# Six equal groups, and the first group's output layer moved in between its input layer's slices

## The chip, the cores and the metric

One core of one Trainium2 chip. The metric is the device time of one execution in microseconds (us); it is quoted as the median of several executions, with the extremes where they matter. The span of a profile, from the first to the last instruction, is 1.75 to 1.8 us shorter than the time of the same execution. Each execution also has a mean granted clock of TensorE (1.0 is full speed).

Engines: PE is TensorE, DVE is VectorE, ACT is ScalarE, POOL is GpSimd, SP is SyncE.

## The reference, cut to what matters

```
state = gamma*state + k[t] (x) v[t];   y[t] = scale * q[t] @ state     # retention, 4 x 8 heads, 768 steps of 64
x = y as (3072, 512)
h = x @ w_in                            # 512 -> 2048
g = h + sin(alpha*h)**2 / (alpha + 1e-9)
out = g @ w_out                         # 2048 -> 512
```

The kernel works in 24 chunks of 128 tokens (4 sequences of 6 chunks). Attention of a chunk has four steps on PE: **T** (transposes of q and k), **A** (scores), **M** (state read and aT times v, into py) and **S** (state update). VectorE copies T's result (qkT), masks A's (aT) and multiplies M's by a decay table (xT). Then come the two layers, for a group of chunks together. The input layer has 16 slices f of 128 columns: four matmuls, a sine and a square, an add (gT). The output layer has 16 matmuls for every chunk, one for each f. I call one such 128x512 matmul an **out**. A group needs its attention before its input layer, and its gT before its outs.

## The kernel before

```python
sizes = [4, 2, 4, 4, 4, 4, 2]                       # chunks in a group

load_w_in(0); load_w_in(1)                          # quarters, some lines put together
load_w_out(0); load_w_in(2); load_w_out(1); load_w_in(3); load_w_out(2); load_w_out(3)

def stage_A(j):
    qkT = st["qkT", j]
    pa = psum.tile([128, 2, NP, 128], F32, name="pa", tag="pa")             # the size of two outs
    ...                                             # eight matmuls
    nc.vector.tensor_mul(aT, pa, mask)              # one mask of 128x1024

def ff_in(g, f, square, cols=None):
    ph = psum.tile([128, hi - lo], F32, name="ph", tag="mm", bufs=4)
    ...                                             # four matmuls
    nc.scalar.activation(out=s, in_=ph, func=ACTF.Sin, scale=alpha_sb[:, f:f + 1])
    if square == "A":
        nc.scalar.activation(out=s, in_=s, func=ACTF.Square)
    else:
        nc.vector.tensor_mul(s, s, s)
    return lambda: nc.vector.scalar_tensor_tensor(gT[g][:, f, lo:hi], s, rec_alpha[:, f:f + 1], ph, ...)

# group 0: three chunks first (f 0 to 5), the fourth chunk e3 in between, with filler matmuls
for f in range(early):
    adds.append(ff_in(0, f, "AADAAA"[f], (0, n3)))
    ...                                             # T, A of e3 between, and dummy matmuls (idle_work)
stage_M(e3)
...
phase(0, [outs of chunk 0], {}, "AD", range(early, FF))
outs = out_pieces(0, (1, 2, 3))                     # the other three chunks' outs: 48
...
# attention of the two chunks of group 1, filled with outs of group 0
fill(7); stage_T(P[4]); scale_v(P[4], nc.vector)
fill(5); stage_A(P[4]); keep_S(P[0], stage_S(P[0]))
fill(5); stage_T(P[5]); scale_v(P[5], nc.vector)
fill(5); stage_A(P[5]); stage_M(P[4])
fill(6); stage_M(P[5]); fill(3)
phase(1, outs, {...}, "A")                          # group 1 (two chunks), the last 19 outs, attention of group 2
```

Of the kernel before, what the change touches and what calls it, by code (L numbers as in the profile page):

```python
# [15 lines left out]
def kernel(  # L16
# [29 lines left out]

    order = [b * NCH for b in range(B)]
    order += [b * NCH + c for b in range(B) for c in range(1, NCH)]
    sizes = [4, 2, 4, 4, 4, 4, 2]
    assert sum(sizes) == NJ  # L50
    NG = len(sizes)
    groups = [order[sum(sizes[:g]):sum(sizes[:g + 1])] for g in range(NG)]
# [37 lines left out]
    def load_w_in(i):  # L90
        nc.gpsimd.dma_start(out=w_in[:, :, i * fw:(i + 1) * fw], in_=w_in_v[:, :, i * fw:(i + 1) * fw])

    def load_w_out(i):
        nc.gpsimd.dma_start(out=w_out[:, i * fo:(i + 1) * fo, :], in_=w_out_v[:, i * fo:(i + 1) * fo, :])
# [16 lines left out]
    def scale_v(j, eng):  # L111
        eng.tensor_mul(raw["v", j], raw["v", j], kg[:, j % NCH, :, None].to_broadcast([128, H, D]))  # L112
# [2 lines left out]
    load_chunk(order[1])  # L115
    load_chunk(order[2])
    load_w_in(0)
    load_w_in(1)
    load_chunk(order[3])
    load_w_out(0)  # L120
    load_w_in(2)
    load_w_out(1)
    load_w_in(3)
    load_w_out(2)
    load_w_out(3)
    for j in order[4:7]:
        load_chunk(j)

# [35 lines left out]
    def decay_table(c):  # L164
        nc.vector.tensor_mul(qg[:, c], qg[:, 0], step[:, c, :, None].to_broadcast([128, NP, C]))
# [24 lines left out]
    def stage_T(j):  # L190
        pt = psum.tile([128, 2 * NP, 128], BF16, name="pt", tag="ty")
        st["qkT", j] = work.tile([128, 2 * NP, 128], BF16, name="qkT", tag="qkT", bufs=6)
        for i in range(2):
            for p in range(NP):
                nc.tensor.transpose(pt[:, i * NP + p, :],  # L195
                                    raw["qk"[i], j][:, 2 * p:2 * p + 2, :].rearrange("p h d -> p (h d)"), ident)
        nc.vector.tensor_copy(st["qkT", j], pt)  # L197
# [3 lines left out]
        st["qkT", j] = work.tile([128, 2 * NP, 128], BF16, name="qkT", tag="qkT", bufs=6)  # L201
        nc.sync.dma_start_transpose(out=st["qkT", j], in_=raw["qk", j].rearrange("p i h d -> p (i h d)"))

    def stage_A(j):
        qkT = st["qkT", j]
        pa = psum.tile([128, 2, NP, 128], F32, name="pa", tag="pa")
        for p in range(NP):
            for e in range(2):
                r = slice(64 * e, 64 * e + 64)
                nc.tensor.matmul(pa[:, e, p, :], qkT[r, NP + p, :], qkT[r, p, :],  # L210
                                 start=(p == 0), stop=True, skip_group_check=True)
        aT = work.tile([128, 2, NP, 128], BF16, name="aT", tag="aT", bufs=2)
        m = dec.rearrange("p e n t -> p (e n) t") if j % NCH == 0 else mask_bc
        nc.vector.tensor_mul(aT.rearrange("p e n t -> p (e n) t"), pa.rearrange("p e n t -> p (e n) t"), m)  # L214
        st["aT", j] = aT

    def stage_S(j):
# [44 lines left out]
    def ff_in(g, f, square, cols=None):  # L262
        n = sizes[g] * C
        lo, hi = cols or (0, n)
        if g not in gT:
            gT[g] = work.tile([128, FF, n], BF16, name="gT", tag="gT", bufs=2)
        ph = psum.tile([128, hi - lo], F32, name="ph", tag="mm", bufs=4)
        s = work.tile([128, hi - lo], F32, name="s", tag="s", bufs=4)
        for i in range(KS):
            nc.tensor.matmul(ph, w_in[:, i, f * 128:(f + 1) * 128], xT[g][:, i, lo:hi],  # L270
                             start=(i == 0), stop=(i == KS - 1))
        nc.scalar.activation(out=s, in_=ph, func=ACTF.Sin, scale=alpha_sb[:, f:f + 1])  # L272
        if square == "A":
            nc.scalar.activation(out=s, in_=s, func=ACTF.Square)  # L274
        else:
            nc.vector.tensor_mul(s, s, s)  # L276
        return lambda: nc.vector.scalar_tensor_tensor(  # L277
            gT[g][:, f, lo:hi], s, rec_alpha[:, f:f + 1], ph, op0=ALU.mult, op1=ALU.add)

# [1 line left out]
    po = {}  # L281
    end = (NG - 1, sizes[-1] - 1)

    def ff_out(g, ts, f):
        if f == 0:
            po[g, ts] = psum.tile([128, d_model], F32, name="po", tag="mm", bufs=4)
        nc.tensor.matmul(po[g, ts], gT[g][:, f, ts * C:(ts + 1) * C], w_out[:, f, :],  # L287
                         start=(f == 0), stop=(f == FF - 1))
        if f == FF - 1:
            o_sb = work.tile([128, d_model], F32, name="o_sb", tag="o_sb", bufs=3)  # L290
            o_dram = out_view[:, groups[g][ts], :]
            if (g, ts) == end:
                h = d_model // 2
                nc.vector.tensor_copy(o_sb[:, :h], po[g, ts][:, :h])
                nc.scalar.copy(o_sb[:, h:], po[g, ts][:, h:])
            else:
                nc.scalar.copy(o_sb, po[g, ts])  # L297
            nc.sync.dma_start(out=o_dram, in_=o_sb)

    def out_pieces(g, tss):  # L300
        return [lambda ts=ts, f=f: ff_out(g, ts, f) for ts in tss for f in range(FF)]
# [5 lines left out]
    def idle_work(n):  # L307
        for _ in range(n):
            nc.tensor.matmul(spare["ps"], warm[:, :128], warm, start=True, stop=True)  # L309
# [47 lines left out]
    def phase(g, outs, att, squares, slots=range(FF)):  # L357

        no, n0, done = len(outs), len(slots), 0
        for n, f in enumerate(slots):  # L360
            add = ff_in(g, f, squares[f % len(squares)])
            for fn in att.get(f, ()):
                fn()
            add()
            while done < no * (n + 1) // n0:
                outs[done]()
                done += 1

    def T(j):
        return lambda: stage_T(j)  # L370

    def X(j):
        return lambda: turn(j)
# [13 lines left out]
    def SK(j):  # L387
        return lambda: keep_S(j, stage_S(j))


    n3, early = 3 * C, 6
    adds = []
    for f in range(early):
        adds.append(ff_in(0, f, "AADAAA"[f], (0, n3)))
        if f == 0:
            decay_table(3)
        if f in (1, 2):
            adds.pop(0)()
        if f == 3:
            idle_work(2)  # L400
            stage_T(e3)
            idle_work(1)
            adds.pop(0)()
        if f == 4:
            stage_A(e3)
            adds.pop(0)()
    idle_work(2)
    adds.pop(0)()
    stage_M(e3)
    adds.pop(0)()  # L410
    idle_work(3)
    for f in range(early):
        add = ff_in(0, f, "AD"[f % 2], (n3, 4 * C))
        if f > 1:
            ff_out(0, 0, f - 2)
        add()
    decay_table(4)
    scale_v(e0, nc.vector)
    for t in s_bd:
        nc.vector.memset(t, 0.0)  # L420
    decay_table(5)
    P = order
    phase(0, [lambda f=f: ff_out(0, 0, f) for f in range(4, FF - 2)], {}, "AD", range(early, FF))
    outs = out_pieces(0, (1, 2, 3))
    outs[9:9] = [lambda f=f: ff_out(0, 0, f) for f in range(FF - 2, FF)]

    def fill(n):
        for _ in range(n):
            outs.pop(0)()


    for n in range(7, NJ + 3):
        if n > 8:
            scale_v(order[n - 3], nc.gpsimd)
        if n < NJ:
            load_chunk(order[n])
        if n in (13, 15, 17):
            scale_v(order[(n - 11) // 2], nc.gpsimd)

    fill(7)  # L440
    stage_T(P[4])
    scale_v(P[4], nc.vector)
    fill(5)
    stage_A(P[4])
    keep_S(P[0], stage_S(P[0]))
    fill(5)
    stage_T(P[5])
    scale_v(P[5], nc.vector)
    fill(5)
    stage_A(P[5])  # L450
    stage_M(P[4])
    fill(6)
    stage_M(P[5])
    fill(3)
    phase(1, outs,
          {0: [T(P[6]), X(P[8])], 2: [A(P[6])], 3: [T(P[7])], 4: [X(P[9])], 6: [A(P[7]), M(P[6])], 8: [X(P[10])],
           10: [A(P[8]), M(P[7])], 12: [X(P[11])], 13: [A(P[9]), M(P[8]), SK(P[9] - 1)], 15: [M(P[9])]}, "A")
    for g in range(2, NG):
        att = {}
        if g + 1 < NG:  # L460
            js = groups[g + 1]
            for i, j in enumerate(js):
                a = i * FF // len(js)
                n = P.index(j) + 2
                if n < NJ:
                    att.setdefault(a + 2, []).append(X(P[n]))
                att.setdefault(a + 1, []).append(A(j))
                if i > 0:
                    att[a + 1].append(M(js[i - 1]))
                if j % NCH == 1:  # L470
                    att[a + 1].append(SK(j - 1))
            att.setdefault(FF - 2, []).append(M(js[-1]))
        phase(g, out_pieces(g - 1, range(sizes[g - 1])), att, "A")
    for fn in out_pieces(NG - 1, range(sizes[-1])):
        fn()


# [1 line left out]
_INS = ['q', 'k', 'v', 'moe_w_in', 'moe_w_out', 'moe_alpha']  # L479
_OUTS = [((3072, 512), 'float32')]  # L480
# [25 lines left out]
```

## Time and profile before

| | before |
|---|---|
| time, median of 4 fast runs beside the changed kernel | 221.68 us (221.38 to 221.96) |
| span of its profile | 220.3 us |
| mean clock of its runs, all studies | 0.995 to 1.0 |
| PE's need, counted from the starts of its matmuls | 192.2 us |

The page of the kernel before cuts the span into 40 slices of 5.5 us; a digit is the busy share in tenths:

```profile
PE   7698889999999999999999999999999999999992
DVE  5586798876896768854565565556554455333300
PEclk9999999999999999999999999999999999999999
```

After the sixth slice (33 us) PE is full everywhere but in the last; DVE is full in two slices only. A stage whose PE is full can still have the chain of another engine hidden below it (from 39.45 to 49.92 us PE is busy for all 10.47 us and VectorE for 8.27), and that is what the change disturbs.

### The profile page before, as it was taken

The numbers are of one execution on the slowest core, as the hardware profiler recorded it, in microseconds if no ns is written. First come the engines' busy times: TensorE is split into PE (matmuls) and PEld (weight loads), VectorE is DVE, ScalarE is ACT, GpSimd is POOL, SyncE is SP. The second block draws the span as 40 slices with busy tenths as digits, with TensorE's granted clock in tenths as the row PEclk, the third lists the DMA queues.
The fourth block names the chain that finished last, engine by engine and source line by source line (L and its number), as shares of the span: only waits on it lengthen the run. The fifth ranks groups of instructions, "written<-read, shape, count | busy, mean of one in ns | idle before, by whom it ended". The sixth has DMA issues, their size and how long they took to land.

```text
span 220.3 us, 4282 instructions
## 1 busy us (share of the span) xinstructions
PE 209.3 (95%) x1661; PEld 106.9 (49%) x1661; DVE 132.3 (60%) x218; ACT 164.8 (75%) x322; POOL 90.1 (41%) x105
## 2 busy tenths in 40 slices
PE   7698889999999999999999999999999999999992
PEld 2444433457664545544455444445444444556540
DVE  5586798876896768854565565556554455333300
ACT  7678777538999999798778778778768877777720
POOL 8965336899999989779510000000000000000000
PEclk9999999999999999999999999999999999999999
DMA  9999999999999999999994145145111101111121
GB/s 127 154 193 191 207 207 163 152 201 155 170 151 145 156 149 185 125 162 175 160 128 71 27 95 72 28 97 74 24 49 51 48 0 51 48 48 48 52 89 54
DMA packets 99509, 24.67 MB, mean 112 GB/s; under 512 B 92304, under 2 KB 96416, under 8 KB 99488
## 3 DMA queue, kind: packets, MB, share of 16 engines
q0 software_dynamic: 77024, 13.37, 83.5%
q1 hardware_dynamic: 22464, 11.02, 26.1%
q8 instruction: 13, 0.21, 0.4%
q14 instruction: 8, 0.07, 0.1%
HBM read 27.27 MB, written 6.29 MB: 152 GB/s over the span
## 4 chain that ended last, share of the span: by engine, by line
PE 79%; DVE 9%; ACT 6%; DMA 2%; issue 2%; SPq 0%; ACTq 0%
PE po L287 36%; PE ph L270 32%; PE pa L210 3%; DVE aT L214 3%; DVE gT L277 3%; PE py L244 3%; ACT s L272 3%; PE py L248 2%; DMA k<-in_k_dram 2%; ACT s L274 2%; PE spare L309 1%; PE ps L224 1%; DVE s L276 1%; DVE xT L255 1%; PE pt L195 1%
## 5 line engine op out<-in xcount | busy, mean ns | idle before, releaser
L277 DVE SCALAR_TENSOR_TENSOR gT<-s,rec_alpha,ph 128x512 bf16<-128x512 f32 (+3 forms) x118 | 75.7, 645 | 67.1 <-ACT s L274 66.3
L287 PE MATMUL po<-w_out,gT 128*128 128x512 bf16 x384 | 101.9, 380 | 1.3 <-DVE gT L277 0.9
L270 PE MATMUL ph<-xT,w_in 128*128 128x512 bf16 (+3 forms) x472 | 101.5, 339 | 1.3 <-DVE gT L277 0.7
L272 ACT ACTIVATE s<-ph,alpha_sb 128x512 f32<-128x512 f32 (+3 forms) x118 | 71.3, 606 | 31.9 <-PE ph L270 31.9
L270 PEld LDWEIGHTS <-w_in 128*128 128x128 bf16 x472 | 45.4, 98 | 46.3 <-issue 4.6
L274 ACT ACTIVATE s<-s 128x512 f32<-128x512 f32 (+3 forms) x109 | 60.3, 553 | 3.5
L287 PEld LDWEIGHTS <-gT 128*128 128x128 bf16 x384 | 35.5, 98 | 38.4 <-DVE gT L277 4.1
L112 POOL TENSOR_TENSOR vr<-vr,kg 128x512 bf16<-128x512 bf16 x21 | 22.2, 1067 | 8.5 <-DMA vr<-in_v_dram 8.5
L214 DVE TENSOR_TENSOR aT<-pa,mask 128x1024 bf16<-128x1024 f32 x20 | 24.4, 1221 | 0.1
L83 POOL DMA_DIRECT2D vr<-in_v_dram x24 | 21.7, 905 | 3.3 <-DMA w_in<-in_moe_w_in_dram 1.7
L83 POOL DMA_DIRECT2D qkr<-in_q_dram x23 | 21.3, 927 | 3.7 <-DMA w_out<-in_moe_w_out_dram 1.6
L83 POOL DMA_DIRECT2D qkr<-in_k_dram x23 | 20.4, 888 | 3.7 <-DMA w_out<-in_moe_w_out_dram 3.3
L297 ACT COPY o_sb<-po 128x512 f32<-128x512 f32 x23 | 13.2, 574 | 6.2 <-PE po L287 6.1
L231 ACT CAST s_bd<-ps 64x256 bf16<-64x256 f32 x40 | 14.4, 360 | 3.5 <-PE ps L224 2.9
L255 DVE TENSOR_TENSOR xT<-py,qg 128x512 bf16<-128x512 f32 x20 | 13.7, 684 | 2.3 <-PE py L248 2.2
L309 PE MATMUL spare<-warm 128*128 128x512 bf16 x36 | 11.4, 430 | 1.2 <-DVE warm L131 1.2
L210 PE MATMUL pa<-qkT 64*128 64x128 bf16 x192 | 9.5, 219 | 0.7 <-DVE qkT L197 0.3
L210 PEld LDWEIGHTS <-qkT 64*128 64x128 bf16 x192 | 5.4, 94 | 9.6 <-issue 6.8
L248 PE MATMUL py<-aT,vr 128*64 128x128 bf16 x192 | 9.5, 219 | 0.5 <-DVE rec_alpha L347 0.2
L244 PE MATMUL py<-qkT,s_bd 128*64 128x128 bf16 x160 | 8.3, 225 | 0.2 <-DVE xT L255 0.2
L248 PEld LDWEIGHTS <-vr 128*64 128x64 bf16 x192 | 6.9, 110 | 1.5 <-issue 1.1
L244 PEld LDWEIGHTS <-s_bd 128*64 128x64 bf16 x160 | 5.2, 109 | 4.0 <-issue 1.9
(58 smaller groups left out, 70.0 us busy)
## 6 DMA issues: line engine op xcount, KB each, us to landing
out_dram<-o_sb SPq DMA_DIRECT2D x24, 256.0 KB, 2.3
vr<-in_v_dram POOLq DMA_DIRECT2D x24, 128.0 KB, 7.5
qkr<-in_q_dram POOLq DMA_DIRECT2D x23, 128.0 KB, 7.8
qkr<-in_k_dram POOLq DMA_DIRECT2D x23, 128.0 KB, 7.7
w_in<-in_moe_w_in_dram POOLq DMA_DIRECT2D x4, 512.0 KB, 11.0
w_out<-in_moe_w_out_dram POOLq DMA_DIRECT2D x4, 512.0 KB, 14.7
q<-in_q_dram SPq DMA_DIRECT2D x1, 256.0 KB, 3.4
k<-in_k_dram SPq DMA_DIRECT2D x1, 256.0 KB, 4.9
```

What stands on the lines that cost most here:

```text
L83: nc.gpsimd.dma_start(out=t, in_=chunk_of(src, j))
L112: eng.tensor_mul(raw["v", j], raw["v", j], kg[:, j % NCH, :, None].to_broadcast([128, H, D]))
L210: nc.tensor.matmul(pa[:, e, p, :], qkT[r, NP + p, :], qkT[r, p, :], start=(p == 0), stop=True, skip_group_check=True)
L214: nc.vector.tensor_mul(aT.rearrange("p e n t -> p (e n) t"), pa.rearrange("p e n t -> p (e n) t"), m)
L244: nc.tensor.matmul(py[r, p, :], s_bd[c % 2][:, p, r], qkT[:, p, :], start=(p == 0), stop=True, skip_group_check=True)
L248: nc.tensor.matmul(py[64 * e:64 * e + 64, p, :], vs[:, 2 * p + e, :], aT[:, e, p, :], start=(c == 0 and p == 0), stop=True, skip_group_che ...
L255: nc.vector.tensor_mul(x, py, qg[:, c])
L270: nc.tensor.matmul(ph, w_in[:, i, f * 128:(f + 1) * 128], xT[g][:, i, lo:hi], start=(i == 0), stop=(i == KS - 1))
L272: nc.scalar.activation(out=s, in_=ph, func=ACTF.Sin, scale=alpha_sb[:, f:f + 1])
L274: nc.scalar.activation(out=s, in_=s, func=ACTF.Square)
L277: return lambda: nc.vector.scalar_tensor_tensor(gT[g][:, f, lo:hi], s, rec_alpha[:, f:f + 1], ph, op0=ALU.mult, op1=ALU.add)
L287: nc.tensor.matmul(po[g, ts], gT[g][:, f, ts * C:(ts + 1) * C], w_out[:, f, :], start=(f == 0), stop=(f == FF - 1))
```

## The change

Its intent: equal groups of four, so that every weight load of PE serves 512 columns; the outs of group 0 directly behind the slices f that they need, in tiles of PSUM (the pool to which both kernels let PE write; one for a 128x512 fp32 result is called a bank here) that attention will only want later; half of group 1's squares on GpSimd, so that ScalarE has room. The core of it:

```diff
-    sizes = [4, 2, 4, 4, 4, 4, 2]
+    sizes = [4] * 6
-    load_w_out(0); load_w_in(2); load_w_out(1); load_w_in(3); ...
+    load_w_out(0) ahead of e3; then w_out and w_in quarters by turns
-            nc.vector.tensor_mul(s, s, s)
+            (nc.vector if square == "D" else nc.gpsimd).tensor_mul(s, s, s)
-    ... f 0 to 5 for three chunks, T(e3), A(e3) and dummy matmuls between, M(e3) ...
+    own = (0, 1, 2)
+    wide = psum.tile([128, 2, d_model], F32, name="wide", tag="pa")          # attention's banks
+    po[0, 0], po[0, 1] = wide[:, 0], wide[:, 1]
+    for f in range(4):
+        ff_in(0, f, "ADAD"[f], (0, n3))()
+    po[0, 2] = psum.tile([128, d_model], F32, name="po", tag="ps")
+    F(own, range(4))                                                         # twelve outs
+    for f in range(4, 7):
+        ff_in(0, f, "AAAD"[f % 4], (0, n3))()
+    stage_T(e3)
+    add = ff_in(0, 7, "A", (0, n3))
+    stage_A(e3, apart=True)                                                  # two half masks
+    add()
+    stage_M(e3)
     ...                                                                      # f 0 to 7 of e3 alone
+    for f in range(8, FF):
+        add = ff_in(0, f, "AD"[f % 2]); add()
+        if f > 9:
+            F(own, (f - 2,))                                                 # three outs in a slot
-    fill(7); stage_T(P[4]); ...; fill(6); stage_M(P[5]); fill(3)             # 31 outs, two chunks
-    phase(1, outs, {...}, "A")                                               # 19 outs
+    ... T, A, M of P[4] to P[7], three decay tables, 22 outs ...             # four chunks
+    phase(1, [], att, "AP")                                                  # no outs, every second square on POOL
```

(The loads of later chunks and their scales on GpSimd also move, some of them into group 1 and group 2. Cut.)

## The prediction

> **What bounds the kernel now.** I began with the chain of waits (PE holds 79% of it, VectorE 9%, ScalarE 6%) and then cut the span at the places where the program changes stage, to see how much of each stage TensorE (PE) really needs. First number of a row: its length; then busy time of PE, weight loads, VectorE (DVE), ScalarE (ACT) and GpSimd (POOL).
>
> ```profile
> 15.62:39.45 23.83, 21.27 (x134) 10.00 (x134) 19.64 (x37) 17.66 (x35) 11.65 (x15) 1.00 1.65 189
> 39.45:49.92 10.47, 10.47 (x121) 5.73 (x121) 8.27 (x11) 4.22 (x10) 9.68 (x11) 1.00 2.25 178
> 49.92:67.87 17.95, 17.38 (x228) 12.08 (x227) 14.82 (x26) 16.31 (x42) 17.45 (x20) 1.00 2.00 156
> 67.87:93.73 25.86, 25.44 (x216) 12.41 (x216) 18.11 (x24) 22.56 (x40) 23.66 (x26) 1.00 2.10 154
> 93.73:216.20 122.47, 122.46 (x865) 60.86 (x863) 61.16 (x85) 92.00 (x168) 14.17 (x15) 1.00 0.54 72
> ```
>
> Busy PE overlaps its own drain, so I count starts instead. In the chain from 94 us on, four 128x512 matmuls repeat every 0.865 us (0.216 each). From the timeline of 41 to 50 us, start to start: eight transposes (T) 0.45, eight score matmuls (A) 0.325, eight state-read matmuls 0.25, eight aT·v matmuls 0.22, eight state updates (S) 0.225.
>
> So the program needs of PE: input layer 384 x 0.2163 = 83.1, output layer the same, attention 26.1: 192.2 us. The last matmul starts its drain near 216.2, so 24 us are lost: 12.6 before the first input-layer matmul at 15.62, then (length minus need) 23.8 - 17.9 = 6.0 in group 0's layers, 10.5 - 10.1 = 0.4 in the filled attention stage, 17.9 - 16.0 = 1.9 in the group of two chunks, 25.9 - 24.9 = 1.0 after it, 2 in the remaining 122. Only about 9 us (6.0+0.4+1.9+1.0) lie where the change works.
>
> The stage from 39 to 50 us carries the argument. Two chunks' attention, on VectorE:
>
> ```profile
> 42.00 0.68 DVE L197 COPY qkT<-pt 128x1024 bf16<-128x1024 bf16 x1
> 42.60 0.68 DVE L112 TENSOR_TENSOR vr<-vr,kg 128x512 bf16<-128x512 bf16 x1
> 43.24 1.22 DVE L214 TENSOR_TENSOR aT<-pa,mask 128x1024 bf16<-128x1024 f32 x1
> 45.11 0.69 DVE L197 COPY qkT<-pt 128x1024 bf16<-128x1024 bf16 x1 [0.65 <-PE pt L195]
> 45.72 0.68 DVE L112 TENSOR_TENSOR vr<-vr,kg 128x512 bf16<-128x512 bf16 x1
> 46.52 1.23 DVE L214 TENSOR_TENSOR aT<-pa,mask 128x1024 bf16<-128x1024 f32 x1
> 47.66 0.68 DVE L255 TENSOR_TENSOR xT<-py,qg 128x512 bf16<-128x512 f32 x1
> 49.18 0.69 DVE L255 TENSOR_TENSOR xT<-py,qg 128x512 bf16<-128x512 f32 x1 [0.84 <-PE py L248]
> ```
>
> It takes about 8 us for two chunks: copy, scale, mask, multiply, each waiting for PE and PE for it. PE lost nothing only because 32 output-layer matmuls (6.9 us) stood between. Costs elsewhere, by group:
>
> ```profile
> L277 DVE SCALAR_TENSOR_TENSOR gT<-s,rec_alpha,ph 128x512 bf16<-128x512 f32 x61 | 45.3, 745 | 38.2 <-ACT s L274 37.8
> L272 ACT ACTIVATE s<-ph,alpha_sb 128x512 f32<-128x512 f32 x61 | 41.9, 687 | 19.7 <-PE ph L270 19.7
> L274 ACT ACTIVATE s<-s 128x512 f32<-128x512 f32 x56 | 35.3, 630 | 1.8
> L112 POOL TENSOR_TENSOR vr<-vr,kg 128x512 bf16<-128x512 bf16 x21 | 22.2, 1067 | 8.5 <-DMA vr<-in_v_dram 8.5
> ```
>
> Independent neighbours overlap by some 0.08 us, so I charge 0.66 for the final add (gT), 0.60 for a sine, 0.53 for a square, 1.14 for a mask, 0.60 for copy, scale and multiply.
>
> [...] this trace shows only the cold start (nine warm-up matmuls in 3.59 us, 0.4 each). [...] the bf16 row above (1067 ns against 0.68 us on VectorE) is less apart, and I estimate 1.1 us for the new fp32 square. [...]
>
> **Part by part.**
>
> *Weights by turns.* From the trace's DMA packets a weight quarter takes 2.55 us and a chunk 2.55; they land in issue order. Before, w_in quarters 0 to 3 landed at 14.7, about 17, 24.9, 30.0, w_out at 22.4 to 35. After, by the same pitch: w_out 0 at 17.3, w_in 1 at 19.8, e3's q and k at 21.5, w_out 1 at 24.9, w_in 2 at 27.5, w_in 3 at 32.5. None delays the walk below; worth nothing by itself, but it permits the early output layer.
>
> *Group 0, f by f.* All starts before 15.62 stay. f 0 to 3 are 384 wide: PE 15.6 to 18.2; their adds on VectorE end at 18.3, 19.4, 19.9, 21.0, so twelve outs end at 21.7. f 4 to 6 then occupy PE until 23.7, T(e3) until 24.1, f 7 until 24.75. But T's copy stands on VectorE behind the add of f 6, whose sine and square (1.03 a pair on ScalarE from 22.6) end at 25.8: copy 26.4 to 27.0, A(e3) 27.0, two half masks until 28.7. PE idles 2.25 + 1.5 us; the filler matmuls that stood here are gone. Outs of f 4, 5 to 30.3, the late column work and outs 6, 7 to 33.35, f 8 to 10 to 35.95, a wait for the add of f 8 to 36.55, then 1.51 us a slot (0.865 + 3 outs) to 44.7, with 42 outs done. Need: 13.8 + 9.1 + 1.0 = 23.9 of 29.1, lost 5.2. Before did 14 outs by 39.45; the 28 more are 6.1 us, so equal work would be 45.5: gain 0.8.
>
> *Attention of four chunks with 22 outs.* VectorE has its last add until 46.4. From then, in program order: scale e0 0.6, two clears 0.55, four copies 2.4, two scales 1.2, three decay tables 1.8, four masks 4.6, four multiplies 2.4: 13.5 us. To that come waits that nothing fills: copy to A to mask, twice 0.5; T(P6) may not use the shared bank before the multiply of P4, 0.65; M(P7) after the multiply of P6, 0.95: 2.6. So 46.4 + 13.5 + 2.6 = 62.5, and the first matmul of group 1 at about 63.0. Cross-check: before needs 8 us for two chunks. PE needs here 22 x 0.216 + 1.8 + 1.3 + 2.8 + 0.2 = 10.9 of 18.3: lost 7.4 against 0.4.
>
> *Group 1, no outs.* PE needs 16 x 0.865 + 4 x (0.325 + 0.695 + 0.1) = 18.3; VectorE 16 x 0.66 + 4 x 1.74 = 17.5; ScalarE 16 x 0.6 + 8 x 0.53 + 4 x 0.74 = 16.8; GpSimd eight squares at 1.1, seven load issues at 0.9, four scales at 1.04: 19.3, of which one scale can run early. All four are nearly full, and PE follows with four ph banks. GpSimd takes its work in order: the square of f 3 waits behind two load issues, and VectorE's mask of P8 stands behind the add of f 3. Walking it: pipeline fill 2.4, that wait 1.5, two or three more of half a microsecond, then the last multiply at 85.8 to 86.4, on which group 2's first matmul depends. Group 1 takes 23.5 us; lost 5.2 against 1.9 in the small group and 1.0 after it.
>
> *From there.* Input layer 16 chunks 55.4, output layer 20 chunks 69.2, attention of 12 chunks 11.8 + 12 x 0.095 for its gaps, 1.0 unexplained as before, tail 4.1 (216.2 to 220.3): 142.6. 86.5 + 142.6 = 229.1; the median of before lies 1.3 above its span, so 230.4. Change in losses: -0.8 + 7.0 + 2.3 = +8.5, and 221.6 + 8.5 = 230.1: the two sums agree.
>
> My errors here lean to waits that overlap in truth, so I take 228.5.
>
> **Rivals.** (1) *PE-bound as intended*: with no stall from 15.62 on, group 0 would end at 39.6, attention be hidden to about 52, group 1 take 18.5: 214 us. For it: a layout tuned in its details and 9 us of loss to win. Against: no engine but PE is free between 46 and 86, and the removed outs were the filler. (2) *The e3 gap filled, the rest as walked*: if the copy slipped ahead of the adds, 3 us less, 226; the program order on VectorE forbids it. (3) *GpSimd squares slower*: at twice my 1.1 us, GpSimd would hold group 1 for 28 us: 234. The bf16 row speaks against twice. (4) *PE falls cold* in the e3 gap (0.3 us of work in 3.9)[...]. (5) *Weights late*: hidden by 2 us everywhere, nothing.
>
> **Range and chances.** Group 0's end is good to 1.5 us, the attention stage to 1, group 1 to 2; together about 3, with a longer tail to the good, where overlap could be underestimated: 223 to 232. Slower by over 2% begins at 226.05: 0.75. Within 2%: 0.20. Faster by over 2% needs 217.2, 9 us below the walk: 0.05.
>
> **What would show it.** In the profile after: PE idle about 24.8 to 28.8 before A(e3) and M(e3), released by VectorE's qkT and aT; 42 outs done near 44.7; VectorE nearly full from 45 to 63 and PE needing 60% of that; first matmul of group 1 near 63, of group 2 near 86; VectorE's adds in group 1 waiting for POOL; from group 2 on the chain of before, and squares on POOL near 1.1 us. I am wrong if group 1 starts before 58, if group 1's stage is under 20 us, or if group 2 starts before 80.

86.5 + 142.6 = 229.1, and 1.3 on top made 230.4, taken as 228.5. The 1.1 us of the fp32 square is an estimate from the bf16 row of 1067 ns. Two remarks on how engines work can be seen in the traces. "Overlaps its own drain": in before four 128x512 matmuls from 93.73 us stand as busy for 1.03 us, and the next four begin 0.86 after them (94.59). "Takes its work in order": in after the sine of f 3 ends at 68.69, but GpSimd's square of it begins at 69.76, behind two load issues begun at 67.94 and 68.87.

## The result, and the profile after

The changed kernel takes 232.87 us in the median of four runs (230.95, 232.03, 233.71, and one of 236.70 that counts as slow, being over 1.5% above the fastest), the kernel before 221.68 beside it. The ratio of fast runs is 1.0476 (95% interval 1.0397 to 1.0556): slower. A ratio here is always the mean time of one kernel's fast runs over the mean of the other's fast runs of the same rounds, so it is not quite the ratio of the medians quoted. The median lies 0.87 us above the predicted range. It is taken over all four runs, the slow one too; over the three fast ones it is 232.03.

The execution that was profiled is the fastest, 230.95 us, with a span of 229.2 and a clock of 0.996. Its 40 slices (5.7 us each):

```profile
PE   7999498876687968999999999999999999999992
DVE  4755729797836996456655645745664734434000
PEclk9999999999999999999999999999999999999998
```

PE has a hole in the fifth slice, and is thin in most slices from the seventh to the sixteenth (34 to 92 us), where DVE is at 9 by turns. After that the kernel is the old one. The same stages as in the prediction's first fence, with the same columns (length; then busy time of PE, PEld, DVE, ACT, POOL; granted clock, DMA share, GB/s):

```profile
15.62:45.00 29.38, 24.76 (x164) 12.84 (x166) 17.58 (x33) 18.31 (x36) 15.98 (x19) 1.00 1.82 183
45.00:63.00 18.00, 11.46 (x180) 6.95 (x182) 15.68 (x21) 5.18 (x12) 8.59 (x9) 1.00 1.68 119
63.00:86.50 23.50, 19.11 (x201) 10.19 (x199) 17.71 (x24) 18.68 (x34) 17.98 (x19) 1.00 0.98 97
```

In the attention stage (second row) PE is busy 11.5 of 18 us and DVE 15.7. In group 1 all four engines are at 17.7 to 19.1 of 23.5, none full. The timeline of PE (start, length, what; in brackets how long it was idle before, and who released it) shows the hole at chunk e3, the waits before the scores of chunk P4, and the first matmuls of groups 1 and 2:

```profile
26.46 0.40 PE L213 MATMUL pa<-qkT 64*128 64x128 bf16 x8 [2.13 <-DVE qkT L196]
27.63 0.22 PE L255 MATMUL py<-aT,vr 128*64 128x128 bf16 x1 [0.78 <-DVE aT L218]
28.23 0.38 PE L255 MATMUL py<-aT,vr 128*64 128x128 bf16 x7 [0.38 <-DVE aT L218]
...
44.60 0.61 PE L194 MATMUL pt<-ident,qkr 128*128 128x128 bf16 x8
46.40 0.39 PE L316 MATMUL wide<-w_out,gT 128*128 128x512 bf16 x1 [1.20 <-DVE gT L284]
47.47 0.59 PE L316 MATMUL wide<-w_out,gT 128*128 128x512 bf16 x2 [0.67 <-ACT o_sb L326]
...
48.73 0.40 PE L213 MATMUL pa<-qkT 64*128 64x128 bf16 x8 [0.24 <-ACT o_sb L326]
...
63.89 1.46 PE L277 MATMUL ph<-xT,w_in 128*128 128x512 bf16 x5 [0.66 <-DVE xT L262]
...
86.77 1.02 PE L277 MATMUL ph<-xT,w_in 128*128 128x512 bf16 x3 [1.15 <-DVE xT L262]
```

The row at 44.60 is T of chunk P4, the row at 48.73 its A. T is the first work after group 0's f loop, which has left 42 outs done. Between 24.3 and 28.6 PE works for a microsecond only. The squares on GpSimd, as a group (count, busy time, mean in ns, idle before), and in the view of waits (us in total, times, longest):

```profile
L283 POOL TENSOR_TENSOR s<-s 128x512 f32<-128x512 f32 x8 | 8.3, 1043 | 13.3 <-ACT s L279 13.2
...
DVE gT L284 <- POOL s L283: 3.1, 4, 1.4
```

VectorE waited four times for them, 3.1 us together.

### The profile page after: what moved, and what is told of

The parts are those of the page before. It is cut to its first block, busy times and chain, and to the rows that moved or that the text cites. A ratio compares the mean times of both kernels' runs of the same rounds, so it can differ in the third digit from the quotient of the medians.

```text
span 229.2 us, 4058 instructions
## 1 busy us (share of the span) xinstructions
PE 205.2 (90%) x1570; PEld 101.9 (44%) x1597; DVE 130.4 (57%) x203; ACT 153.3 (67%) x282; POOL 98.5 (43%) x113
## 4 chain that ended last, share of the span: by engine, by line
PE 67%; DVE 14%; POOL 8%; ACT 4%; DMA 3%; issue 3%; POOLq 0%; DVEq 0%; ACTq 0%
PE po L316 31%; PE ph L277 27%; DVE gT L284 3%; DMA w_in<-in_moe_w_in_dram 3%; POOL qkr L83 3%; DVE aT L221 3%; PE pa L213 2%; POOL s L283 2%; PE py L251 2%; DVE xT L262 2%; ACT s L279 2%; PE wide L316 2%; POOL vr L83 2%; PE py L255 1%; DVE qkT L196 1%
## 5 line engine op out<-in xcount | busy, mean ns | idle before, releaser
L284 DVE SCALAR_TENSOR_TENSOR gT<-s,rec_alpha,ph 128x512 bf16<-128x512 f32 (+1 forms) x96 | 69.8, 734 | 68.1 <-ACT s L281 64.4
L277 PE MATMUL ph<-xT,w_in 128*128 128x512 bf16 (+1 forms) x376 | 93.3, 375 | 3.4 <-DVE xT L262 1.8
L316 PE MATMUL po<-w_out,gT 128*128 128x512 bf16 x337 | 87.5, 379 | 1.7 <-issue 1.3
L279 ACT ACTIVATE s<-ph,alpha_sb 128x512 f32<-128x512 f32 (+1 forms) x96 | 64.4, 676 | 35.8 <-PE ph L277 35.0
L277 PEld LDWEIGHTS <-w_in 128*128 128x128 bf16 x384 | 37.2, 98 | 46.0 <-issue 3.0
L281 ACT ACTIVATE s<-s 128x512 f32<-128x512 f32 (+1 forms) x82 | 51.0, 622 | 2.6
L326 ACT COPY o_sb<-po 128x512 f32<-128x512 f32 x21 | 12.0, 572 | 8.3 <-PE po L316 8.3
L283 POOL TENSOR_TENSOR s<-s 128x512 f32<-128x512 f32 x8 | 8.3, 1043 | 13.3 <-ACT s L279 13.2
L316 PE MATMUL wide<-w_out,gT 128*128 128x512 bf16 x29 | 8.9, 381 | 3.0 <-DVE gT L284 2.4
L338 PE MATMUL spare<-warm 128*128 128x512 bf16 x27 | 9.4, 469 | 1.3 <-DVE warm L130 1.2
```

The costliest lines, as they stand in the source:

```text
L277: nc.tensor.matmul(ph, w_in[:, i, f * 128:(f + 1) * 128], xT[g][:, i, lo:hi], start=(i == 0), stop=(i == KS - 1))
L316: nc.tensor.matmul(po[g, ts], gT[g][:, f, ts * C:(ts + 1) * C], w_out[:, f, :], start=(f == 0), stop=(f == FF - 1))
```

## The experiments

Fifteen runs were made, of fourteen further kernels and of the changed one again, all with correct results; each beside runs of the kernel before on the same chip. I write the kernel before as "before" and the changed one as "after".

### 1. Why do runs of one kernel differ by 5 us? (again, fillers, fillers_all)

Theory: the half-clock state of PE, which the prediction held as a rival only, occurs in some runs. First the unchanged kernel after, six runs:

> The changed kernel once more, to see its scatter. Theory C (a part of the runs loses TensorE clock because the kernel now leaves TensorE idle for 1 to 2 us at a time): runs spread again from about 230.5 to 235, each slow one with a mean granted clock of 0.97 to 0.985, while the kernel before stays within 0.3% at 0.998. Rival D (the first scatter was an accident of that one session): all runs near 231 with a clock of 0.995 or more.

Measured: 233.54 us in the median (232.04 to 236.49), ratio 1.0495 (1.0451 to 1.0539). The profiled run has half clock directly behind the hole at e3. The rows are 2 us each, the granted clock is the third number from the right:

```profile
26.00:28.00 2.00, 0.40 (x8) 0.33 (x9) 1.51 (x3) 0.82 (x2) 0.85 (x1) 1.00 1.23 205
28.00:30.00 2.00, 1.35 (x9) 0.74 (x10) 1.37 (x3) 0.48 (x1) 0.88 (x1) 0.59 1.24 206
30.00:32.00 2.00, 1.78 (x8) 0.74 (x7) 0.00 (x0) 0.11 (x1) 0.88 (x1) 0.56 1.24 206
32.00:34.00 2.00, 2.00 (x31) 1.65 (x29) 0.00 (x0) 1.04 (x4) 0.35 (x1) 1.00 1.29 203
```

In nine profiles that were cut into steps of 1 us, twelve such stretches last 3.40 to 3.42 us by their clock, and three (tables_early once, two_group_new twice) 6.82. In fillers the steps have 0.75, 0.50, 0.50, 0.54, which is 3.42 us at half. One of them lowers the mean clock of a 230 us run by 0.5 x 3.4 / 230 = 0.0074. So the clock of a run counts its stretches: 0.996 to 1.0 is none, 0.99 one, 0.984 two, 0.977 three, 0.97 four. This is worked out, not seen, for the runs without a profile; in the profiled ones the clock records agree with it. The ten runs of after, sorted by it:

| stretches | clock | times (us) | mean |
|---|---|---|---|
| 0 | 0.996, 0.997 | 230.95, 232.03 | 231.5 |
| 1 | 0.989 to 0.993 | 232.98, 232.04, 232.16 | 232.4 |
| 2 | 0.983, 0.984 | 233.71, 234.11 | 233.9 |
| 3 | 0.976 | 234.66 | 234.7 |
| 4 | 0.969, 0.971 | 236.70, 236.49 | 236.6 |

Each costs about 1.3 us (from 231.5 us without to 236.6 with four). In what follows the runs called slow have three to five by their clocks; the kernel before, whose longest wait of PE after 15.62 us is 0.95 us, against 2.13 and 1.82 in after, had by its clocks (0.995 to 1.0) none in any run.

Of the time just ahead of five of these stretches the windows view says: PE was busy for 0.50 of 3.41 us (again), 1.58 of 3.41 (own_two), 1.60 of 3.40 (e3_first), 1.18 of 3.41 (fillers) and 1.33 of 3.45 (own_one), so 15 to 47%. A hole like that does not always bring one: in after PE was busy for 0.61 of the 3.41 us from 24.82 on, at the same hole at e3 as in again, and no stretch followed. In the five of the nine profiles that show more than one stretch, their starts lie 3.0 (old_loads), 4.0 and 7.0 (two_group_new), 6.0 (own_two), 7.0 (tables_early) and 17.0 (own_one) times 3.41 us apart. Why a stretch follows in one run and not in another is not shown.

If the holes cause it, dummy matmuls in the holes remove it without changing anything else. **fillers**: 39 of them, by the edit (the expectation says 36), at the waits between 24 and 64 us.

```diff
     stage_T(e3)
     add = ff_in(0, 7, "A", (0, n3))
+    spare["ps"] = psum.tile([128, 512], F32, name="spare", tag="mm", bufs=4)
+    idle_work(9)                                   # 128x512 matmuls on zeros
     stage_A(e3, apart=True)
     add()
+    idle_work(5)
     stage_M(e3)
 ...                                                # and 5, 8, 3, 3, 3, 3 in the attention stage
```

> The changed kernel with 36 dummy matmuls put back into its idle gaps between 24 and 64 us (e3's scores, and the attention of four chunks), no real work changed. Theory C: clock 0.995 or more in every run, all times within 0.5% of 231, median about 231.0. Rival D (clock dips have another cause): the same spread as in the plain repeat, and the same median to 0.5 us. Neither theory expects the fastest run to move by more than 0.7 us.

Measured: 232.01 (231.13 to 232.90), ratio 1.0434 (1.0398 to 1.0471). The clock is 0.997 or 0.998 in three runs and 0.991 or 0.992 in three: none or one stretch, where after had up to four. The one in its profile begins at 87 us, after the holes at the end of group 1 that I had left open. **fillers_all** fills these too (14 more dummies, behind f 13 and around the last M of group 1):

```diff
+            att[13] = att.get(13, []) + [fresh]                     # a bank and 4 dummies
+            att[FF - 1] = [fresh] + att[FF - 1] + [lambda: idle_work(6)]
```

> The kernel of run fillers with 14 more dummy matmuls near the end of group 1, where PE still has gaps of 1 to 1.5 us. Theory (the spread of the changed kernel's runs, and the 2 us by which its median lies above its cleanest run, are stretches at half clock that follow gaps): clock .996 or above in every run, spread under 1 us, median about 231.2, that is the fastest runs of fillers. Rival (the clock drops from another cause): clocks .991 in half the runs and a spread of 2 us as in fillers, median 232.

Measured: clocks 0.996 to 1.0 in all six runs, 231.31 to 232.28 us, median 231.80, ratio 1.0451 (1.0424 to 1.0477). The spread is 0.97 us, where the same kernel without dummies had 4.5 us. The median came 0.6 above what I expected. The stretch of 26 to 32 us in its profile:

```profile
26.00:28.00 2.00, 1.65 (x14) 0.63 (x14) 1.51 (x3) 0.20 (x1) 0.32 (x2) 1.00 1.24 207
28.00:30.00 2.00, 1.98 (x18) 1.04 (x18) 0.73 (x2) 0.58 (x1) 0.67 (x1) 1.00 1.24 205
30.00:32.00 2.00, 2.00 (x31) 1.65 (x29) 0.00 (x0) 1.02 (x4) 0.87 (x1) 1.00 1.24 206
```

So the scatter and 1.1 to 1.7 us of the median (232.87 and 233.54 against 231.80) are half-clock stretches behind holes of PE. The other 10 us are not: without any stretch the kernel is still 4.5% slower.

### 2. The hole at e3 (e3_first)

VectorE takes its work in order, and the copy of e3's T stood behind the adds of f 4 to 6: in after T ends at 23.68 us, the adds begin at 23.14, 24.16 and 25.19, the copy at 25.72. This experiment puts T, A and M of e3 in front of them:

```diff
+    stage_T(e3)
+    add4 = ff_in(0, 4, "A", (0, n3))
+    stage_A(e3, apart=True)
+    add5 = ff_in(0, 5, "A", (0, n3)); stage_M(e3); add4()
+    ...                                            # f 6, 7, and the adds behind
```

> The changed kernel with e3's transposes, scores and attention moved in front of the adds of f 4 to 7, so that VectorE's copy does not stand behind the add of f 6. Theory (the e3 gap is VectorE's program order, and everything after it follows PE): group 0's last out comes at about 42 in place of 44.6, and since the attention stage after it is a chain of its own, the end moves by the same 2.5: fastest run about 228.5. Rival (the late column work and the adds behind it then become the bound): under 1 us gained.

Measured: 229.57 (229.03 to 231.59), ratio 1.0349 (1.0303 to 1.0394); span of the profile 227.3. PE's wait before A(e3) is gone, group 0 ends at 42.58 instead of 44.60. A caution for this and every other stage end: the first input-layer matmul comes between 14.7 and 15.6 us in the profiles (14.93 and 15.61 in the two of after's own kernel), so the ends of a stage in two single profiles can differ by that alone. Counted from that matmul, group 0 takes 27.40 us here and 29.67 in after. The order of instructions at e3 is thus worth 2.0 to 2.3 us in group 0's end, and 2.4 between runs with one stretch (mean 229.9 against 232.4 of after). Every run has one such stretch (0.991 to 0.993), in the profile at 47 us, so the fastest was 229.03 and not 228.5. Most of the loss remains.

### 3. The grouping and the early outs apart (six_groups, two_group_new, two_group_b)

**six_groups** is before with the new grouping only: the 64 outs stay as fillers (14 in group 0, 33 in the attention of four chunks, 17 in group 1), the squares on ScalarE, the loads as before.

```diff
-    sizes = [4, 2, 4, 4, 4, 4, 2]
+    sizes = [4] * 6
+    stage_T(P[6]); fill(3); stage_A(P[6]); fill(4); stage_T(P[7]); fill(2); ...   # two chunks more
-    phase(1, outs, {...}, "A")
+    phase(g, outs if g == 1 else out_pieces(g - 1, ...), att, "A")
```

> The kernel before with only the grouping changed to six groups of four: group 0 and the weights' order as before, attention of four chunks filled with 33 of group 0's outs, 17 left for group 1, squares on ScalarE. Theory (the loss of the change is the missing filler, not the grouping): attention stage 39.5 to about 53.5 with TensorE losing under 1 us, group 1 about 22.3, group 2's first matmul at about 76, time about 219.5, 1% under the kernel before. Rival (four chunks in a row or groups of four are themselves the loss): group 2's first matmul later than 80, time above 224.

Measured: 225.11 (224.74 to 225.44), ratio 1.0131 (1.0101 to 1.0161), span 223.0, clocks 0.996 to 1.0. Group 1 starts at 56.42, group 2 at 80.58. Its two stages:

```profile
39.45:56.40 16.95, 14.17 (x200) 8.41 (x201) 13.17 (x17) 5.55 (x14) 16.11 (x19) 1.00 2.13 156
56.40:82.00 25.60, 23.82 (x213) 11.84 (x216) 18.04 (x24) 23.45 (x43) 24.38 (x27) 1.00 2.26 156
```

I missed on both sides: the grouping alone costs 3 us, less than the rival and more than nothing. Before group 1 can start, the attention of eight chunks is needed, where before needed that of six, with the same 64 outs to fill it; attention's stage loses 2.8 us of PE, and in group 1 ScalarE is nearly full (23.45 of 25.6).

Set beside after, this run shows where the early outs went. The two differ in the order of outs, the squares, the loads and the place of VectorE's tables, not in the grouping:

| stage | six_groups | after | longer by | outs in it, less by |
|---|---|---|---|---|
| to the end of group 0 | 39.45 | 44.60 | 5.15 | -28 (more) |
| attention of four chunks, to group 1's first matmul | 16.97 | 19.29 | 2.32 | 11 (2.4 us of PE) |
| group 1, to group 2's first matmul | 24.16 | 22.88 | -1.28 | 17 (3.7 us of PE) |
| rest | 142.4 | 142.4 | 0 | 0 |

The sum is 6.2, and 229.2 - 223.0 = 6.2. The 28 outs taken out of the later stages were 28 x 0.216 = 6.05 us of PE work; those stages became longer by 1.0 in sum. They were not waiting for PE. Part of what they wait for can be seen behind group 0's end: from T(P4) to the scores A(P4) after takes 4.13 us (44.60 to 48.73) and six_groups 1.78 (40.85 to 42.63). In after PE waits there for the add of f 15 (1.20 us) and for ScalarE to copy early outs out of attention's banks (0.67 and 0.24). VectorE's tables, which after has in this stage and six_groups in group 0, are weighed in experiment 6.

**two_group_new** is the other corner: after, with the old grouping. Group 0 as changed, then attention of two chunks with its 22 outs, the group of two without outs, the loads of before.

```diff
-    sizes = [4] * 6
+    sizes = [4, 2, 4, 4, 4, 4, 2]
+    ... T, A, M of P[4] and P[5] with 6 + 16 outs; then the old phase 1 without outs, and the old loads
```

> The changed kernel with its groups set back to 4, 2, 4, 4, 4, 4, 2: group 0 f by f as changed, then attention of two chunks with its 22 outs, the group of two without outs, and the loads of the kernel before. With six_groups this completes the square of grouping and output order. Theory A (grouping and early outs want the same few filler matmuls, so together they cost more than apart): group 0 ends at 44.6 again, the attention stage of two takes about 9 us, the group of two 16.5 to 17.5, so group 2 starts at 70 to 71 and the span is about 223, time about 225; then grouping costs 6 us with early outs and 3 without. Rival B (the two parts simply add): grouping costs 3 in either case, span 226, time 228. Rival C (the early outs themselves are the harm): span 228 or more, time 230.

Measured: 230.96 to 237.40, median 232.70, ratio 1.0462 (1.0415 to 1.0508), clocks 0.964 to 0.984: nothing near 225. The profile (a slow run) shows why it cannot be used. Instructions of VectorE took two to three times their usual length while GpSimd was running. First VectorE, then GpSimd:

```profile
47.97 2.30 DVE L283 TENSOR_TENSOR s<-s 128x512 f32<-128x512 f32 x1
60.92 3.58 DVE L164 TENSOR_TENSOR qg<-qg,step 128x512 f32<-128x512 f32 x3
```
```profile
47.91 1.09 POOL L112 TENSOR_TENSOR vr<-vr,kg 128x512 bf16<-128x512 bf16 x1
48.90 0.94 POOL L83 DMA_DIRECT2D qkr<-in_q_dram  x1
62.62 2.78 POOL L112 TENSOR_TENSOR vr<-vr,kg 128x512 bf16<-128x512 bf16 x2
```

Such a square otherwise takes 0.69, three such tables 1.82 to 1.89 (before, tables_early). Two GpSimd scales took 2.78 instead of 2.08. In after too a scale of VectorE, begun at 47.96 inside GpSimd's two scales of 46.60 to 48.84, took 1.44 instead of 0.68. The square began 0.06 us behind a GpSimd scale of 1.09 us and took 1.61 us more than usual; how much of that is owed to the scale, and how much to the load issue that followed, is not shown. Beside load issues alone both was seen: in after a bf16 scale of VectorE took 1.20 us instead of 0.68 at 51.05 us, while GpSimd had only load issues running (50.60 to 54.10 us), and in two_group_new the same scale took 0.69 at 50.97 beside a load issue of 50.70 to 51.60. Behind the lengthened instructions of two_group_new come holes of PE and half-clock stretches, some 10 us of these after 51 us.

**two_group_b** repeats the corner with the loads placed as in after.

```diff
-    for n in range(7, NJ + 3): ...                 # the old loop, all loads at once
+    the load and scale order of the changed kernel, through the group of two (amid) and group 2 (rest)
```

> As two_group_new, but with the load order of the changed kernel behind group 0 and through the group of two: in two_group_new the old load loop ran on GpSimd while VectorE did its last square and three decay tables, which took 2.30 and 3.58 us instead of 0.69 and 1.9, and the profile showed five windows at half clock. Theory (VectorE stretched by GpSimd's load issues, and the cold clock after it, hid the corner): the attention stage takes 10 to 12 us instead of 17.5, group 2 starts near 73 in a clean run, span 224 to 225, time 226 in the best run. Rival (early outs leave too little filler for the group of two as well): 229 to 231 as two_group_new's best run.

Measured: 228.26 and 229.55 in the fast runs (clock 0.991 to 0.992, one stretch), 233.04 and 233.69 in the slow ones (0.97); before 222.16 beside it. No interval was had, with two fast runs. The profiled run, 228.26, has span 226.5; its only stretch lies in group 0 (the first row's 0.95):

```profile
14.77:45.90 31.13, 26.67 (x159) 13.87 (x162) 17.50 (x33) 18.18 (x36) 15.79 (x19) 0.95 1.84 181
45.90:56.25 10.35, 7.95 (x107) 4.80 (x108) 9.36 (x15) 3.62 (x9) 9.62 (x10) 1.00 1.19 137
56.25:74.02 17.77, 13.76 (x212) 10.79 (x211) 16.98 (x29) 16.53 (x43) 12.84 (x14) 1.00 1.83 160
```

The attention stage ends with the first matmul of the group of two, at 56.80: 10.9 us for two chunks with 22 outs, where before takes 10.5 with 31 (32 in the prediction's row, with group 0's last out). The group of two takes 17.2 us without outs, where before takes 17.95 with 19. So 28 outs fewer (6.05 us of PE) shorten these stages by 0.3 us. In both, VectorE is busy for 9.4 of 10.4 and 17.0 of 17.8 us.

The four corners, spans of the profiled runs:

| | outs as fillers | outs early |
|---|---|---|
| 4, 2, 4, 4, 4, 4, 2 | 220.3 (before) | 226.5 with one stretch, about 225.2 without (two_group_b) |
| six of four | 223.0 (six_groups) | 229.2 (after) |

The early outs cost 5 to 6 us with either grouping, the grouping 3 to 4 with either order. They add, as rival B of two_group_new had it, to within the 1.3 us of one stretch, below which nothing is resolved here. Theory A, that both want the same filler and cost 3 us more together than apart, falls. (The right column also has the loads by turns, VectorE's tables in the attention stage and, in after, the squares on GpSimd; experiments 5 and 6 have their worth.)

### 4. Outs moved back into attention (own_two, own_one)

If early outs are the harm, moving some back into the attention stage should help. In after, chunks 0 to 2 have their outs early; own_two leaves two of them early, own_one one.

```diff
-    own = (0, 1, 2)
+    own = (0, 1)                                   # own_one: (0,)
-    outs = [lambda f=f: ff_out(0, 3, f) for f in range(FF)]
+    outs = out_pieces(0, (2, 3))                   # own_one: (1, 2, 3)
     ...                                            # 32 fills, own_one 48, in the attention stage
```

> The changed kernel with the output layer of one of the three chunks (16 outs) taken out of group 0's f-by-f stage and put between the steps of the four chunks' attention instead. Theory (the attention stage is a chain through VectorE that hides outs for nothing, and the early outs were its filler): group 0 ends 14 x 0.216 = 3.0 earlier, near 41.6, the attention stage keeps its length of about 19 us, and the fastest run is 228.0. Rival (the stage is bound by the sum of work): stage 3 us longer, fastest run 231.

> The same with two of the three chunks' outs moved back (32 outs, 48 fill the attention stage). Theory: group 0 near 39.5 (then bound by ScalarE and VectorE at about 1.15 us a slot rather than by TensorE), attention stage about 19.5, group 1's first matmul near 59, fastest run 226, and clock dips fewer. Rival: as for the one chunk, 231; or TensorE now bounds the stage (16.5 us of need) and half of the gain is lost, 228.5.

Measured: own_two 232.67 (three runs 232.22 to 232.69 at 0.985, one of 235.44 at 0.969), ratio 1.0513 (1.0448 to 1.0578); own_one 232.65 (231.33 to 234.57, at 0.969 to 0.985), ratio 1.0493 (1.0431 to 1.0555). The medians do not fall. With as many stretches (two) after has 233.9, own_two 232.5, own_one 231.3 and 232.2: some 1.5 to 2 us are gained and given back to more stretches at half clock. That is less than was expected. The stages of own_one:

```profile
14.80:42.41 27.61, 21.39 (x134) 11.08 (x134) 16.93 (x33) 17.68 (x36) 13.71 (x17) 0.94 1.72 185
42.41:62.62 20.21, 17.87 (x220) 10.15 (x219) 16.16 (x23) 5.75 (x14) 10.86 (x12) 1.00 1.43 138
```

Half the thought was right: attention's stage took 32 more outs (6.9 us of PE work) and lasted 20.2 us instead of 19.3. But group 0 became only 2.2 us shorter (42.41 against 44.60, with a stretch at half clock in it). With one out in a slot it takes 1.08 to 1.38 us a slot (1.25 in the mean), though PE needs 0.865 + 0.216 = 1.08, and three outs fit into 1.51: there too some outs are nearly free. The 64 outs of group 0 can be had once, and three stages want them: group 0's second half, attention of four chunks, group 1. In before two stages want them, and shorter ones.

### 5. Loads by turns, and squares on GpSimd (old_loads, squares_act)

```diff
-    for i in range(1, WP): load_w_out(i); load_w_in(i + 1)         # cut
+    load_w_out(0); load_w_in(2); load_w_out(1); load_w_in(3); load_w_out(2); load_w_out(3)
```

> The changed kernel with the weights' load order of the kernel before. Prediction's reading (the turns are worth nothing alone but permit the early output layer): w_out's first quarter lands at about 22.4, so the first twelve outs wait from 17.7 to about 22.4 with TensorE idle, e3 is ready earlier but stands behind them in program order, and the fastest run is about 4 to 5 us slower than the plain change, near 235. Rival (the order does not matter): within 1 us.

Measured: 238.77 (237.80 to 241.00), ratio 1.0796 (1.0737 to 1.0854), 6 us more than after in the median, and 4 to 5 at the same clock. PE waits for w_out before the first early out, and most of its twelve outs then come at 0.43 us each, at half clock:

```profile
23.06 0.59 PE L317 MATMUL wide<-w_out,gT 128*128 128x512 bf16 x2 [4.84 <-DMA w_out<-in_moe_w_out_dram]
```

So loading by turns is what permits early outs, as the prediction said; that it is worth nothing by itself was not tried.

```diff
-        phase(g, ..., att, "AP" if g == 1 else "A")
+        phase(g, ..., att, "A")
```

> The changed kernel with group 1's squares all on ScalarE, none on GpSimd. Theory (group 1 is slow because four chunks' attention shares it with the layer and nothing is left to fill TensorE; GpSimd is one of four nearly full engines): ScalarE then needs 16 x 1.13 + 3.0 = 21 us, group 1 takes 22 to 24 us in place of 22.9, fastest run within 1.2 us of 231. Rival (GpSimd's in-order work is what holds group 1): group 1 under 20 us, fastest run below 228.5.

Measured: 232.45 and 232.68 in the fast runs (0.990 and 0.991), 237.8 in two slow ones; ratio 1.0482 (1.0447 to 1.0518). Group 1 takes 23.5 us (65.01 to 88.53) instead of 22.9, with ScalarE busy for 22.0 of them. The squares on GpSimd therefore gain about 0.6 us in their stage, in spite of the 3.1 us of waits for them; in whole runs with one stretch (232.6 against 232.4) the gain is hardly seen. That GpSimd holds group 1 is refuted.

### 6. Tables, and two repairs together (tables_early, mended)

The three decay tables, a scale and two clears stand on VectorE in the attention stage of after, where it is the bound; VectorE had free time in group 0.

```diff
+    decay_table(3); decay_table(4); decay_table(5)                 # in group 0, where VectorE waited
+    scale_v(e0, nc.vector); clears of s_bd
-    (the same at the end of group 0 and in the attention stage)
```

> The changed kernel with the three decay tables, the scale of e0's v and the two clears (2.95 us of VectorE) moved out of the attention stage into VectorE's 4 us wait before the late columns of group 0. Theory (the attention stage is bound by VectorE's own sum plus a few waits): stage 19.3 becomes about 16.8, group 1's first matmul near 61.3, fastest run about 228.3. Rival (the stage is bound by the chain copy, scores, mask, attention, multiply through the shared bank, and these fillers of VectorE stood in its waits): under 1 us gained.

Measured: 230.27 in its only run without a stretch (clock 0.999), 233.42 to 234.66 in the others, with three each. That is 0.7 below after's best run, and with three stretches 234.0 in the mean against 234.7: the rival's number. Its reason, that these instructions stood in the waits of a chain, does not follow from it, as the next run shows. **mended** is this with e3_first:

> e3's attention moved ahead and the tables moved as well, all else as in the changed kernel. Theory (the two add up, and what is left is the grouping): group 1's first matmul near 59.5 to 60, fastest run about 226, still 2% slower than the kernel before. Rival (these two details were the whole of the loss): 222.5 or less.

Measured: 229.26 (228.45 to 230.56), ratio 1.0339 (1.0292 to 1.0386); expected 226. The attention stage took 17.6 us (43.48 to 61.12) instead of 19.3, so 1.7 of the 2.95 us moved were saved in it. But group 0, counted from its first input-layer matmul, took 28.75 us where e3_first has 27.40: PE's wait for the add of f 8 rose from 0.69 to 1.40, so VectorE's time in group 0 was not free. With one stretch mended takes 229.9 and 230.6, e3_first 229.9 in the mean of four: on top of e3_first the tables gain nothing that these runs resolve, and the two do not add up. A wait of after remains (0.67 and 0.24 us there): A of P4 needs the banks that hold early outs, and these are free only when ScalarE has copied them out.

```profile
46.35 0.59 PE L316 MATMUL wide<-w_out,gT 128*128 128x512 bf16 x2 [0.68 <-ACT o_sb L326]
...
47.61 0.40 PE L213 MATMUL pa<-qkT 64*128 64x128 bf16 x8 [0.24 <-ACT o_sb L326]
```

Its two runs without a stretch (228.45 and 228.66) are 3 us below those of after. With both repairs the kernel is still 3% slower than before: the loss lies in the plan more than in its details.

### 7. Can before be bettered from what was learnt? (po_in_ps, try_best)

Group 0's slots in before take 1.08 to 1.38 us. po_in_ps gives the outs of its chunk 0 the bank of the state, so that the input layer has four banks instead of three:

```diff
+    po[0, 0] = psum.tile([128, d_model], F32, name="po", tag="ps")
```

> The kernel before with one part of the idea alone: the output tile of group 0's first chunk lies in the bank of the attention state (free until then) and not in one of the four banks of the layer's tiles. Theory (group 0's slots of about 1.2 us, with 1.08 of TensorE work, wait for the third and last ph bank): slots of 1.08 to 1.12, about 1 us gained, 221.0 where the kernel before is 222. Rival (they are bound by the sum of VectorE's work): within 0.3 us.

Measured: 221.95 against 221.93, ratio 1.0003 (0.9979 to 1.0027): nothing. The bank does not bind the slots; that sine, square and add do was not tried. try_best has in addition eight early f instead of six (so M(e3) comes earlier), and every third square of the small group on VectorE:

```diff
-    n3, early = 3 * C, 6
+    n3, early = 3 * C, 8
-    phase(1, outs, {...}, "A")
+    phase(1, outs, {...}, "AAD")
```

> The kernel before with that bank, with two more of group 0's f done 384 wide while e3 is on its way (8 in place of 6, in the place of dummy matmuls), and with every third square of the small group on VectorE (ScalarE is busy 16.3 of 17.95 us there). Theory: 1 us from the bank, about 1.2 from the two f (two slots fewer at 1.2, two late ones more at 0.55), 0.4 from the squares: about 219.5, faster than both kernels. Rival: the two f cost ScalarE as much as they save TensorE, 221 or more.

Measured: 223.98 (222.92 to 225.55), ratio 1.0096 (1.0054 to 1.0139). The attention stage ended at 49.11, some 0.8 us earlier than in before, but its first input-layer matmul also came 0.9 earlier (14.70 against 15.62), so the two f gained nothing there, and the small group then took 19.6 us instead of 17.95, VectorE being busy for 17.8 of them. None of these versions beats before.

## Why the prediction was right or wrong

**Direction** was right, and the mechanism in the main. Without filler the stages between 45 and 87 us are bound by chains over VectorE, ScalarE and GpSimd; PE is busy for 11.5 of 18 us in attention.

**The walk**, step by step, against the run without a half-clock stretch: PE idle between 24.8 and 28.8 around A(e3) and M(e3), measured waits of 2.13, 0.78 and 0.38 us ending at 28.6; f loop to 44.7 with 42 outs, measured 44.60; group 1's first matmul at 63.0, measured 63.89; group 1's stage 23.5, measured 22.9; group 2 at 86.5, measured 86.77; a GpSimd square 1.1 us, measured 1.043; span 229.1, measured 229.2. None of these was off by over 1 us, in part by luck. "All starts before 15.62 stay" was not so: the first input-layer matmul came at 14.93, and the stage to 44.60 took 29.7 us, not 29.1. The attention stage's "46.4 + 13.5 + 2.6" has neither the waits for early outs' banks (0.67 and 0.24 us) nor two scales of VectorE that took 1.44 and 1.20 instead of 0.60, and 1.82 instead of 0.65 for the wait of T(P6); the stage took 19.3 us instead of 18.3.

**From the walk to 228.5.** Here it failed, in three terms. First, "My errors here lean to waits that overlap in truth, so I take 228.5": 1.9 us taken off the sum without a row that asked for it, and the sum needed nothing off. Second, the median of before "lies 1.3 above its span" compared a median with one profile; of the same execution it is 1.75 (230.95 - 229.2), so 0.45 was missing. Third, rival (4), that PE falls cold in the e3 gap, was kept as a rival and put into neither the number nor the upper end of the range. The runs show it as a matter of chance: none to four stretches a run, 1.3 us each, and 1.9 us between the cleanest run and the median (232.87 - 230.95), of which fillers_all explains 1.1 (232.87 - 231.80); the rest is scatter among runs without a stretch, as of 230.95 and 232.03. 228.5 + 1.9 + 0.45 + 0.1 + 1.9 = 232.85. By fillers_all the median without stretches would have been about 231.8, just inside the range. The rival also had the place too narrow: behind the holes at 46 and 86 us the same was seen (a stretch from 49.48 us in own_two, from 86.08 in own_one).

**The split of the loss** was booked in a way that the experiments don't bear out. By lost PE time I gave group 0 "f by f" a gain of 0.8, the attention stage a loss of 7.0 and group 1 one of 2.3. The sum is right, but "the 28 more are 6.1 us, so equal work would be 45.5: gain 0.8" values an early out at its full PE time, as if that were saved later. In the later stages it was worth 0.3 us out of 6.05 with the old grouping and a loss of 1.0 with the new one. By corners, the early outs cost 5 to 6 us (2.0 to 2.4 of it the hole at e3) and the grouping 3 to 4.

**The rivals.** PE-bound as intended (1) is refuted by every run. A filled e3 gap (2) was mended in e3_first and gave 2.0 to 2.4 us, not 3. Squares on GpSimd at twice 1.1 us (3) did not come, at 1.043, which is 1.5 times the 0.69 us of the same square on VectorE; that GpSimd binds group 1 is refuted by squares_act. Weights late (5): by turns PE waited for one once, 0.18 us at its first input-layer matmul.

What stays open: how much of the early outs' cost beyond the hole at e3 is group 0's slots, and how much the wait for banks and tables behind it; tables_early puts the tables at 0.7 to 1.2 us, the banks were not tried apart. In which run a hole is followed by half clock is open too; experiment 1 has what the profiles show of it.

## What to carry to other kernels

An instruction that fills a wait can be nearly free where it stands, and cost much of its time where you move it to. Here 28 outs, 6.05 us of PE, were taken out of two stages, which became 0.3 us shorter with the old grouping and 1.0 longer with the new one; group 0, which got them, became 5.15 us longer with the new one, the hole at e3 included. Before moving fillers, ask for each stage what it would take without them (the sum of the busiest engine's durations, and the chain from one engine to the next). When a change opens holes on PE, read the granted clock of every run, not of one profile: a few half-clock stretches shifted the median by 1.1 to 1.7 us here and left the fastest run untouched (230.95 us, against 231.31 with all holes filled). And do not shade a walked sum in a direction for which no row speaks.
